# One loop of single tiles, in place of a tree of conditions, for an expert's tokens past its first 128

## The chip, the cores and the metric

The kernel runs on one core of a Trainium2 chip. The metric is the device time of one execution in microseconds, from the first instruction to the end. Inputs and outputs lie in device memory, and all tokens are routed on the chip.

## The reference

Three parts follow one another. First an attention with a position bias (4 batches, 8 heads, 576 positions, head size 64). Then a dense two-layer network with a SiLU-like gate. Last a mixture of eight experts, and only this part is touched:

```python
do_compute = x @ w_skip > 0                 # 2304 tokens of 512 features
e_idx  = argmax(xc @ w_gate)                # one expert per token
gate_w = softmax(xc @ w_gate)[e_idx]
h      = maximum(xc[mask] @ w1[e], 0)       # 512 -> 1024
y      = gate_w * (h @ w2[e])               # 1024 -> 512
out    = xc + y                             # other tokens: out = x
```

How many tokens an expert gets is known only at run time. The kernel must work for any count.

## The kernel before

All matrix work of the experts is done in pairs of 16-bit numbers: a value is split into a high and a low half (`xh`, `xl`; `Wh`, `Wl`; `hh`, `hl`), and three of the four products are summed. So a tile of 128 tokens takes, for each of eight slices `f` of the hidden layer, twelve matmuls of 128 columns (L547), then a ReLU on ScalarE (L554) and the low half on VectorE (L555), and, two slices later (`MLAG`), three matmuls of 512 columns (L563). With the four transposes of the next expert's tokens (`spread`, L523) that makes 124 matmuls. A matmul is two instructions of TensorE, a weight load and the multiplication.

The stage order is written by hand from `tail` on (`manual_schedule`): each engine runs its instructions in program order. `experts` (L626) goes through the eight experts. The first 128 tokens of an expert are one tile with a hook, `between`, that puts other work between its slices: the previous tile's end (`finish`, L581 and L582: gate and residual on VectorE, then a scatter by POOL into `out`), the fetch of later tokens by POOL (L504), the split of the next expert's weights in eight pieces (`piece`, L497 on ScalarE and L498 on VectorE), and the issue by SP of the loads of later weights (`load`, L481 and L483; two transfers of 256 KB for a piece, into a ring of 16, so a load waits until the piece 16 places earlier has been split). All engines get the expert's count as a number of half tiles, `n[e]` (L648); SP gets it too and takes its own branches, and so runs ahead of the others.

Tokens past the first 128 are handled by a tree of conditions (L669 to L697). `n == 3` runs a half tile (`expert_half`), `n == 4` a second full tile (`second`), `n > 4` fetches three more tiles and runs the second tile with a spread of these, then either a double tile and a half (`n == 9`) or a triple tile and, past ten, a loop over four tiles at a time. For experts 0 and 7 the second tile's tokens are already transposed ahead of the condition (`SY0`, `SY7`). In the listing of the compiled program the tree takes about 1,750 instructions of TensorE for each expert: 241 to 246 for the half tile, as many for the second full tile, 257 to 261, 529 and 338 for the larger ones, and 404 for the loop's body. Where a condition fails, an engine jumps over its block to a few instructions that add to its counters what the block would have counted; POOL does this for its transfers with one counter instruction (INC_SWDGE_SEM) after waiting for its earlier transfers.

A loop over a number known only at run time (`tc.For_i`) is written by the framework as follows, and the loop at L693, which this run does not reach, is in the listing. The first pass is entered directly. Between two passes stands a block in which SP waits for the counters of every engine and of every DMA queue, all five engines meet in a join, each takes back its counters (POOL by the same kind of counter instruction), they meet in a second join, and the body begins again. After the last pass each of the five engines goes through 13 instructions that wait for the counters of all engines and DMA queues, those of earlier loads among them, before it goes on.

## Time and profile before

| | us |
|---|---|
| median of 3 runs (999.99 to 1008.25) | 1003.2 |
| the profiled execution | 1003.57 |
| its span | 1001.5 |
| TensorE busy | 814.1 (81%) |
| VectorE busy | 701.9 (70%) |
| ScalarE busy | 531.4 (53%) |
| POOL busy | 77.1 (8%) |

The profile is one execution. Its page splits the span into 40 slices, the last eight of which hold the experts. Busy time of TensorE (PE) is the time in which a matmul was in its pipeline; PEld is the weight load beside it. A row of a timeline gives start, duration, engine, line, operation, output and inputs, how many instructions were merged, and in brackets the idle time before and what ended it; "PEq L669" there is the branch at L669 on TensorE's sequencer. DVE is VectorE, ACT is ScalarE. A row by stretch gives its start and end, its length, the busy time of PE, PEld, DVE, ACT and POOL with the number of instructions, the granted TensorE clock as a share of full speed, the DMA engines' busy share, and GB/s.

### The profile page before, as it was taken

How to read it: one execution, taken by the hardware profiler on the slowest of the kernel's cores; microseconds unless marked ns; L12 is line 12 of the kernel's file. 1: busy time of each engine (PE TensorE's matmuls, PEld its weight loads, DVE VectorE, ACT ScalarE, POOL GpSimd, SP SyncE). 2: the span in 40 equal slices, each digit the busy share in tenths (PEclk: the TensorE clock that was granted, in tenths of full speed). 3: DMA queues.
4: the chain of work that ended last, by engine and by line, in shares of the span. 5: the costliest groups of instructions: out<-in, count | busy, mean ns of one | idle time of the engine just before them, and what ended most of it. 6: DMA issues, size and time to landing. Idle time of an engine off the chain costs nothing. (4 is left out here: it accounts for less than half of the span.)

```text
span 1001.5 us, 21950 instructions
## 1 busy us (share of the span) xinstructions
PE 814.1 (81%) x8074; PEld 534.0 (53%) x8074; DVE 701.9 (70%) x1989; ACT 531.4 (53%) x1067; POOL 77.1 (8%) x98
## 2 busy tenths in 40 slices
PE   5656598578679999988897999999989775778973
PEld 1212254364375757475745556756674554656652
DVE  6798898889964778677666877776776555672251
ACT  5555566574653657466555656656563344662140
POOL 1110011000000000000000000000001221120010
PEclk9788999799889999999999999999989898788998
DMA  7999999999995899999979998979697769860010
GB/s 195 244 289 262 261 290 220 265 248 253 274 208 111 192 182 221 215 219 203 198 157 181 215 219 189 214 152 205 124 267 234 217 216 291 251 196 13 24 29 15
DMA packets 357238, 199.25 MB, mean 199 GB/s; under 512 B 263900, under 2 KB 319580, under 8 KB 357088
## 3 DMA queue, kind: packets, MB, share of 16 engines
q1 hardware_dynamic: 350112, 178.84, 78.5%
q0 software_dynamic: 6160, 17.97, 6.2%
q8 instruction: 82, 1.34, 0.6%
q10 hardware_dynamic: 816, 0.54, 0.2%
q14 instruction: 68, 0.56, 0.2%
HBM read 113.52 MB, written 24.19 MB: 138 GB/s over the span
## 5 line engine op out<-in xcount | busy, mean ns | idle before, releaser
L280 PE MATMUL hps<-x,win 128*128 128x192 f16 x2304 | 213.3, 251 | 7.3 <-DVE th L284 5.8
L300 PE MATMUL ops<-wout,g 128*128 128x512 f16 x864 | 203.3, 385 | 9.7 <-ACT wout L267 6.8
L280 PEld LDWEIGHTS <-win 128*128 128x128 f16 x2304 | 191.0, 99 | 19.9 <-issue 11.1
L217 ACT ACTIVATE e<-e,st 128x576 f32<-128x576 f32 x144 | 111.0, 771 | 79.7 <-DVE st L215 74.8
L300 PEld LDWEIGHTS <-g 128*128 128x128 f16 x864 | 79.9, 99 | 101.5 <-issue 13.0
L222 DVE SCALAR_TENSOR_TENSOR en<-e,st,en 128x576 f16<-128x576 f32 x144 | 116.9, 815 | 24.1 <-ACT en L221 23.2
L212 PE MATMUL sc<-kT,qT 128*64 128x512 f16 (+1 forms) x1152 | 108.0, 305 | 29.2 <-ACT bs L140 15.2
L221 ACT ACTIVATE en<-e,st 128x576 f16<-128x576 f32 x144 | 110.0, 768 | 27.6 <-ACT e L217 15.3
L215 DVE CUSTOM_DVE_ANT_0 e<-sc,bt 128x576 f32<-128x576 f32 x144 | 108.3, 752 | 18.7 <-PE sc L212 10.3
L547 PEld LDWEIGHTS <-W 128*128 128x128 f16 x1056 | 80.7, 110 | 56.1 <-issue 35.2
L212 PEld LDWEIGHTS <-qT 128*64 128x64 f16 x1152 | 58.7, 114 | 87.5 <-issue 61.0
L235 PE MATMUL av<-eT,vh 128*64 128x192 f16 x864 | 68.2, 253 | 44.5 <-DMA eT<-en 41.9
L137 PE MATMUL bps<-hh,hb 128*32 128x64 f32 (+1 forms) x576 | 77.0, 660 | 26.8 <-ACT bs L140 10.2
L235 PEld LDWEIGHTS <-vh 128*64 128x64 f16 x864 | 50.4, 112 | 55.6 <-issue 37.2
L547 PE MATMUL h<-xh,W 128*128 128x128 f16 x512 | 47.5, 246 | 32.4 <-PEq L669 24.0
L428 POOL DMA_INDIRECT slots<-ent x18 | 19.4, 1077 | 580.5 <-DVE ent L427 458.9
L137 PEld LDWEIGHTS bps<-hh,hb 128*32 128x32 f32 x576 | 19.6, 125 | 82.2 <-issue 50.8
L131 DVE TENSOR_SCALAR hh<-pos 128x576 f32<-128x576 f32 x120 | 55.4, 516 | 7.5 <-PE bps L137 7.4
L288 ACT ACTIVATE g<-th 128x384 f16<-128x384 f32 x96 | 48.4, 514 | 22.6 <-DVE th L284 22.6
L284 DVE SCALAR_TENSOR_TENSOR th<-th,hps 128x384 f32<-128x384 f32 x96 | 52.1, 548 | 7.6 <-ACT th L283 7.2
L289 DVE SCALAR_TENSOR_TENSOR g<-th,g 128x384 f16<-128x384 f32 x96 | 52.2, 552 | 2.8 <-ACT g L288 2.0
L283 ACT ACTIVATE th<-hps 128x384 f32<-128x384 f32 x96 | 45.5, 479 | 14.6 <-PE hps L280 12.2
(150 smaller groups left out, 1080.7 us busy)
## 6 DMA issues: line engine op xcount, KB each, us to landing
bt<-bias_d SPq DMA_DIRECT2D x144, 288.0 KB, 3.5
win<-in_moe_w SPq DMA_DIRECT2D x48, 256.0 KB, 6.3
wout<-in_moe_w SPq DMA_DIRECT2D x46, 256.0 KB, 5.5
bias_d<-bs POOLq DMA_DIRECT2D x36, 288.0 KB, 5.2
wr<-in_moe_w_in SPq DMA_DIRECT2D x16, 512.0 KB, 5.7
wr<-in_moe_w_out SPq DMA_DIRECT2D x16, 512.0 KB, 4.7
qr<-in_q SPq DMA_DIRECT2D x48, 96.0 KB, 3.9
x2s<-x SPq DMA_DIRECT2D x36, 128.0 KB, 2.5
```

Source lines behind the costliest of these rows:

```text
L131: nc.vector.tensor_scalar(hh, src, self.bl[:, j : j + 1], 0.0, op0=ALU.add, op1=ALU.max)
L137: nc.tensor.matmul(ps[32 * c : 32 * c + 32, ks], self.w2b, v.rearrange("q (p n) -> q n p", n=4) if ks.start == 0 else v, start=True, stop= ...
L212: nc.tensor.matmul(o, qT[:, w, i, js], k_, start=(w == 0), stop=(w == 1))
L215: nc.vector.tensor_tensor_reduce(out=e, in0=sc[:, :S], in1=bt, scale=1.0, scalar=3.0e38, op0=ALU.add, op1=ALU.min, accum_out=st4[:, 0:1])
L217: nc.scalar.activation(e, e, AF.Exp, bias=st4[:, 0:1], scale=-1.0, accum_out=st4[:, 1:2])
L221: nc.scalar.activation(en[:, 0], e, AF.Copy, scale=st4[:, 2:3])
L222: nc.vector.scalar_tensor_tensor(out=en[:, 1], in0=e, scalar=st4[:, 2:3], in1=en[:, 0], op0=ALU.mult, op1=ALU.subtract)
L235: nc.tensor.matmul(av[js], v_[:, j, kb], eT[:, :, kb, js], start=(n == 0), stop=(n == len(seq) - 1))
L280: nc.tensor.matmul(ps[:, u], self.win[w][:, k, fs], x[:, k], start=(i == 0), stop=(i == 11))
L289: nc.vector.scalar_tensor_tensor(out=gl, in0=th, scalar=XS / (2 * XS * WS), in1=gh, op0=ALU.mult, op1=ALU.subtract)
L300: nc.tensor.matmul(ps, self.g[gi][:, fb, d], self.wout[w][:, fb, :], start=(n == 0), stop=(n == 47))
L547: nc.tensor.matmul(h, w[:, f, 0, 128 * k : 128 * k + 128], v[:, k], start=(i == 0), stop=(i == 11))
```

## The change

The tree of conditions goes, with `expert_half`, the wide forms of `expert_tile`, the buffers for these (`yb`, `xqb`, `hqb`) and the early spreads of experts 0 and 7. In its place stands one condition with one loop, whose body handles one tile of 128 tokens. Each pass transposes the tokens in `xn`, keeps a copy of them (`xk`) and of their rows and gates (`idk`), loads the next tile's rows from `slots` into `idq`, fetches its tokens into `xn`, computes, and scatters. The high and low halves of the tokens lie side by side in `xc`, so that one matmul of 256 columns multiplies a weight by both; the two results are added by a copy on ScalarE and an addition on VectorE. With the transposes a pass has 92 matmuls, 184 instructions of TensorE.

```diff
-        self.yb = [m.tile([128, 4, 128], F16, name=f"y{i}", bufs=1) for i in range(2)]
...
+        at = lambda o, n, dt: g1[:, o : o + n].bitcast(dt)
+        self.more = (m.tile([128, 2], I32, name="idq", bufs=1), m.tile([128, 2], I32, name="idk", bufs=1), at(0, 1024, F32),
+                     g1[:, 1024:2048].rearrange("p (k v c) -> p k v c", k=4, v=2), [at(2048 + 256 * i, 256, F32) for i in range(3)],
+                     *([g1[:, 2816 + 128 * (2 * i + v) : 2944 + 128 * (2 * i + v)] for i in range(3)] for v in range(2)))
...
+    def expert_more(self, e, ids, n, xn):
+
+        nc, tc, m = self.nc, self.tc, self.m2
+        Wh, Wl = self.W[e]
+        idq, idk, xk, xc, hs, hh, hl = self.more
+        j = 2 * (e * SL + 1)
+        slots = self.slots.rearrange("(p n) c -> p (n c)", p=128)
+        with tc.If(n > 2):
+            nc.vector.tensor_copy(idq, ids[:, j : j + 2])
+            with tc.For_i(2, n, 2) as i:
+                xp = self.ps.tile([128, 1024], F32, tag="sc", name="xp", bufs=SCB)[:, :512].rearrange("p (k c) -> p k c", k=4)
+                for k in range(4):
+                    nc.tensor.transpose(xp[:, k], xn[:, 128 * k : 128 * k + 128], self.ident)
+                nc.scalar.activation(xc[:, :, 0], xp, AF.Copy, scale=XS)
+                nc.vector.scalar_tensor_tensor(out=xc[:, :, 1], in0=xp, scalar=XS, in1=xc[:, :, 0], op0=ALU.mult, op1=ALU.subtract)
+                nc.gpsimd.tensor_copy(xk, xn)
+                nc.gpsimd.tensor_copy(idk, idq)
+                nc.gpsimd.dma_start(idq, slots[:, ds(i + j, 2)])
+                self.fetch1(idq[:, 0:1], xn)
+                y = self.ps.tile([128, 1024], F32, tag="sc", name="y", bufs=SCB)[:, :DM]
+                for f in range(8 + MLAG):
+                    if f < 8:
+                        h = self.ps.tile([128, 2, 128], F32, tag="mm", name="h", bufs=MMB)
+                        for k in range(4):
+                            nc.tensor.matmul(h, Wh[:, f, 0, 128 * k : 128 * k + 128], xc[:, k], start=(k == 0), stop=False)
+                        for k in range(4):
+                            nc.tensor.matmul(h[:, 0], Wl[:, f, 0, 128 * k : 128 * k + 128], xc[:, k, 0], start=False, stop=(k == 3))
+                        q = f % 3
+                        nc.scalar.activation(hs[q], h[:, 1], AF.Copy)
+                        nc.vector.tensor_tensor(hs[q], h[:, 0], hs[q], op=ALU.add)
+                        nc.scalar.activation(hh[q], hs[q], AF.Relu)
+                        nc.vector.scalar_tensor_tensor(out=hl[q], in0=hs[q], scalar=0.0, in1=hh[q], op0=ALU.max, op1=ALU.subtract)
+                    if f >= MLAG:
+                        g, q = f - MLAG, (f - MLAG) % 3
+                        for p, w in ((hh, Wh), (hh, Wl), (hl, Wh)):
+                            nc.tensor.matmul(y, p[q], w[:, g, 1], start=(g == 0 and p is hh and w is Wh), stop=(g == 7 and p is hl))
+                nc.vector.scalar_tensor_tensor(out=xk, in0=y, scalar=idk[:, 1:2].bitcast(F32), in1=xk, op0=ALU.mult, op1=ALU.add)
                 nc.gpsimd.indirect_dma_start(
+                    out=self.out, out_offset=bass.IndirectOffsetOnAxis(ap=idk[:, 0:1].bitcast(U32), axis=0),
+                    in_=xk, in_offset=None, bounds_check=NT - 1, oob_is_err=False)
...
@@ experts
-                if e in (0, NE - 1) and f == (SY7 if e else SY0):
-                    st["y"] = self.spread([xm[e]], "y")
...
-            with tc.If(n[e] > 2):
...
-            st.pop("y", None)
+            self.expert_more(e, ids, n[e], xm[e])
```

## Rows read from the trace of the kernel before

**Rows 1.** Stages of the experts: length, busy us by engine, granted clock, DMA share

```profile
796.20:811.77 15.57, 10.88 (x120) 7.66 (x121) 4.52 (x11) 2.63 (x9) 3.25 (x4) 1.00 0.84 265
811.77:833.36 21.59, 12.74 (x125) 9.38 (x126) 12.29 (x18) 9.81 (x18) 5.87 (x5) 0.87 0.76 236
...
869.81:888.88 19.07, 14.03 (x124) 10.31 (x125) 12.40 (x18) 10.36 (x18) 2.92 (x3) 0.77 0.87 258
...
902.08:950.65 48.57, 41.86 (x401) 29.96 (x401) 13.34 (x30) 9.10 (x25) 2.97 (x3) 0.93 0.05 18
950.65:969.54 18.89, 13.14 (x124) 9.30 (x125) 13.12 (x19) 9.94 (x17) 4.56 (x4) 0.91 0.14 39
969.54:980.52 10.98, 10.98 (x124) 8.14 (x125) 3.03 (x9) 2.82 (x9) 0.00 (x0) 1.00 0.02 4
980.52:1001.50 20.98, 5.68 (x121) 4.11 (x119) 3.41 (x7) 1.11 (x4) 1.89 (x2) 0.76 0.05 17
```

**Rows 2.** Branches and counters by line: count, ns min/median/max; TensorE's waits

```profile
L669 PEldq COMPARE_BRANCH  x8: 70/4250/6136, 794.9 to 979.1; - x8
...
L669 POOLq INC_SWDGE_SEM  x5: 1478/1602/1902, 826.4 to 963.0; - x5
...
  PE h L547: 24.0, 5
...
L673 PEldq COMPARE_BRANCH  x4: 71/270/353, 795.0 to 984.2; - x4
...
L675 PEldq COMPARE_BRANCH  x4: 68/205/3135, 796.4 to 984.4; - x4
```

**Rows 3.** Timeline of TensorE at the start of expert 3

```profile
851.52 0.98 PE L547 MATMUL h<-xh,W 128*128 128x128 f16 x8 [4.59 <-PEq L669]
...
855.81 0.61 PE L547 MATMUL h<-xh,W 128*128 128x128 f16 x8
```

**Rows 4.** VectorE's groups from 850 us on: count, busy us, mean ns, idle

```profile
L498 DVE SCALAR_TENSOR_TENSOR W<-wout,W 128x1024 f16<-128x1024 f32 x16 | 19.5, 1221 | 7.4 <-ACT W L497 7.1
...
L555 DVE SCALAR_TENSOR_TENSOR hl<-h,hh 128x128 f16<-128x128 f32 x40 | 11.5, 288 | 11.3 <-ACT hh L554 11.3
L581 DVE SCALAR_TENSOR_TENSOR g<-y,ids,g 128x512 f32<-128x512 f32 x8 | 5.9, 750 | 6.1 <-PE y L563 5.7 <-PEq L690 0.4
...
L526 DVE SCALAR_TENSOR_TENSOR xl<-xp,xh 128x512 f16<-128x512 f32 x4 | 2.7, 683 | 0.0
```

**Rows 5.** Timeline of SP, first of 14 issues up to 802.37

```profile
793.46 0.38 SPq L481 DMA_DIRECT2D wout<-in_moe_w  x1
```

**Rows 6.** One stretch of 10 us, columns as in the first group

```profile
840.00:850.00 10.00, 6.85 (x65) 4.28 (x61) 7.05 (x11) 4.70 (x9) 1.69 (x2) 1.00 1.04 316
```

**Rows 7.** Timeline of all engines in expert 0's second tile

```profile
795.91 0.58 POOL L642 DMA_DIRECT2D ids<-slots  x1 [2.04 <-DMA slots<-ent]
...
797.09 1.56 PE L547 MATMUL h<-y,W 128*128 128x128 f16 x25 [0.91 <-DVEq L673]
...
801.82 0.99 POOL L504 DMA_INDIRECT g<-x2s,ids  x1 [5.33 <-DMA ids<-slots]
```

**Rows 8.** Issue to landing: of the fetch L504, then the scatter L582

```profile
DMA to landing us min/median/max: 3.3/4.3/7.0
...
DMA to landing us min/median/max: 2.2/3.1/5.8
```

**Rows 9.** Timeline of TensorE at the start of expert 5's second tile

```profile
905.97 0.88 PE L523 MATMUL xp<-ident,g 128*128 128x128 f32 x4 [3.88 <-PEq L675]
907.58 4.00 PE L547 MATMUL h<-y,W 128*128 128x128 f16 x36 [0.74 <-ACT y L525]
```

**Rows 10.** POOL's groups over the span, columns as for VectorE's

```profile
L345 POOL MEMSET sen<- 128x352 int32 x1 | 0.4, 392 | 0.0
```

**Rows 11.** Timeline of POOL at the end

```profile
988.05 0.91 POOL L622 DMA_INDIRECT out<-g,ids  x1 [5.31 <-DVEq L675]
```

## The prediction

> **What bounds the kernel now.** I read the chain of waits first. It goes back only a few experts and names little but "issue", so I went on to a table by stage [rows 1] and to each stage's timeline. The change touches only the last 205 us, where the eight experts run one behind the other. Each expert streams one tile of 128 tokens: 124 matmuls, 10.98 us where nothing disturbs them (969.54 to 980.52). Experts 1 to 4 take 77.1 us together (811.77 to 888.88; four stages, first and last shown, 21.59 and 19.07 us). VectorE is busy for only about 12 us of each, and the DMA engines for 0.76 and 0.87 of it, so neither fills a stage. What ends the idle time on TensorE is the branch of the outer `If` (L669): five waits, 24.0 us [rows 2]. That branch lasts 70 ns where it falls through (the minimum) and 4.25 (the median of all eight) to 6.14 us where it is taken and jumps over the whole tree, some 1,750 TensorE instructions in the listing of the program. After such a gap TensorE is granted the lower clock for a while: eight matmuls take 0.98 us at 851.52 and 0.61 us at 855.81 [rows 3]. From 851.52 to 855.81 it does three groups of twelve matmuls of 128 columns and one of three of 512. A tile at the full clock has eight of each, 1,536 columns a group, and the transposes in 10.98 us: 0.66 us a group, 2.6 for four. About 1.6 us are lost.

> Which experts have more than 128 tokens is read from the stages: expert 0 runs a second full tile (n = 4, 15.57 us), expert 5 the branch n = 9 (48.57 us), expert 7 a half tile (n = 3). The other five skip. So the change is a trade: five cheaper skips against one, four and one passes of the new loop.

> **Skips, experts 1 to 4.** The new block holds 92 matmuls, 184 TensorE instructions and about 30 for the loop's ends, so the skip jumps some 215. The nearest rows are L673 and L675, which jump over 241 to 246: 0.2 to 0.35 us, once 3.14 us, right behind another jump [rows 2]. I take 0.4 us, and 3.1 us as the upper bound. With the gap gone VectorE sets the pace: per expert 8 pieces of 1.22 us, 8 hl of 0.288, one xl of 0.683 and one finish of 0.750, 13.5 us [rows 4]; with hand-overs I take 14.0. The clock then stays up, except in expert 1, which follows a loop: 14 x 4 + 1.5 = 57.5 us against 77.1, a gain of 19.6.
> What could be late next is the weights. SP, which ran ahead, now has to join expert 0's loop. The seven pieces it issued from 793.46 on (the row is the first of 14 issues [rows 5]) go out only after that loop, and 24 more must land before expert 5's tile ends: 31 x 0.524 MB = 16.2 MB. At the 316 GB/s of one 10 us stretch [rows 6] that is 51 us, at the 258 GB/s of a whole stage 63. There are some 70 us until then, so I take nothing, and 5 us as the bound, since each expert's share has its own due time.

> **Expert 6.** Its stage of 18.89 us holds one skip of about 4 us and a slow start; at VectorE's pace it becomes 15: a gain of 3.9.

> **Expert 0's pass.** The first instruction in the new block is VectorE's copy of `idq` out of `ids`. That transfer is issued at 795.91 and lands 5.7 us later; today only POOL's fetch waits for it, until 801.82 [rows 7]. VectorE works in order, so the low half of xc stands behind this copy, and every first matmul reads both halves. Today the second tile starts at 797. Now: copy until 802.0, xc 0.68, start at 802.7. The body streams the same columns as a tile does (per f: 4 x 256 + 4 x 128 for 12 x 128), 10.5 us without the transposes, plus 1.8 at the low clock: 815.0. Then 0.2 + 0.75 (gate) + 0.25 until POOL's scatter starts, 2.7 until it lands (the scatter's row has 2.2 to 5.8, median 3.1, beside heavy traffic [rows 8]; without SP's loads I take below the median), and the exit, where every engine goes through 13 waits: 1.0. That is 819.9 against 811.77: a loss of 8.2. Removing the early spread of xm saves under 0.5 us of TensorE.

> **The cost of a pass.** No loop runs in the trace of before, so its join is bounded. What hides nothing: the next pass may not start until the scatter has landed, since the join waits for all DMAs. Per pass: lead 2.3 us (transposes at 905.97 to the first matmul at 907.58 are 1.6 [rows 9], plus 0.68 for the low half that this body needs at once); body 10.5; low clock 1.6; gate and hand-overs 1.2; landing 2.7; join 3.3. The join is one POOL counter instruction of 1.48 to 1.90 us [rows 2], which stands between the two joins, and 1.7 for SP's row of waits and both joins. Low bound 1.5 (that instruction alone), high bound 5. Sum 21.6 us.
> POOL's copy of xn has no row; POOL's largest plain write takes 0.39 us [rows 10], and I allow 0.4 to 3. The load of idq (5.7 at most, by the row of `ids`) and the fetch of the next tile (1.0, and 4.3 to land [rows 8]) follow it. That makes 11 to 14 us beside the 14 of lead, body and low clock, so nothing, or 1 us a pass. The four small operations per f (ScalarE, VectorE, ScalarE, VectorE, each within 0.29) make a chain of 1.3 us, while its reader comes 1.3 to 2.6 us later: nothing, at most 1 us a pass.

> **Expert 5.** First pass 20.6 (little low clock), three of 21.6, less 2.3 because the last ends in the exit: 83.1 us against 48.57, a loss of 34.5. The matmuls themselves hardly grow (41.9 us busy now, 44 then); the loss is four leads, three joins, four landings.

> **Expert 7.** From 980.52 to its scatter at 988.05 [rows 11] it takes 7.5 us; then 0.1 + 2.0 + 10.5 + 1.2 = 13.8. A loss of 6; what follows the scatter I leave as it is (a join comes, two counter instructions go).

> **Sum.** -19.6 - 3.9 + 8.2 + 34.5 + 6.0 = +25.2 us. The profiled execution took 1003.57 us (span 1001.5), 0.4 above the median of the three runs, so 1003.2 + 25.2 = 1028.

> [...] On the rows, a jump over 1,750 instructions costs 4 to 6 us and one over 245 mostly 0.2 to 0.35 [rows 2]. [...] No run here shows a jump back; what it would do is the first rival.

> **Rivals.**
> *Fetches stay* (0.18). TensorE's jump back reaches for code that has gone, and short skips cost what L675's dearest did. For: that row's maximum. Against: the medians of both rows of short jumps. Price: five skips x 2.7 = 13.5. A fetch at a jump back of 3.1 to 6.1 us runs beside the 4 to 7 us of gate, landing and join, so 3 x 1.5 = 4.5. 1028 + 18 = 1046.
> *Cheap joins* (0.13). Each landing at 2.2, join at 1.5, no low clock: 3.9 less in three of expert 5's passes, 1 to 2 less in each of the other three, experts 1 to 4 at 13.5: about -17, 1011.
> *Passes overlap: faster or level* (0.09). Place: the end of a pass in expert 5. If an engine could go on before the scatter has landed, the transposes of the next tile and POOL's fetch would run behind the gate, and a pass would cost lead and body, 13.5. Expert 5: 4 x 13.5 + 3 = 57 (+8.5); expert 0 without landing and exit +4.5; expert 7 +5; against -23.5: -5.5, 998. With the pace at VectorE's bare 13.5 us and a shorter lead it comes under 993. It decides where a pass falls below 15 us. Against: the joins wait for every DMA.

> **Numbers.** Forecast 0.60 (its own range 1016 to 1040), and 0.18, 0.13, 0.09 for the three. About 1% (993 to 1013) is what a measurement here can tell from no change. Faster: 0.05, out of the overlap. Within: 0.10, 0.04 of the overlap and 0.06 of the cheap joins. Slower: 0.85. The range 1010 to 1046 takes in the bounds of join, landing and fetch.

> **What would show it.** The five skips at 0.2 to 0.5 us, and experts 1 to 4 at 14 us each with VectorE over 90% busy. TensorE idle for 7 to 10 us between expert 5's passes, ended by a join, with starts 21 to 22 us apart. Expert 0's first loop matmul at 802 to 803. Expert 7's scatter 14 us after its tile. The forecast is wrong if the passes are under 15 us apart, if the skips still cost 3 us, or if ScalarE or VectorE waits in experts 2 to 4 for weights.

## The result: slower by 1.0%, where 2.5% was forecast

The changed kernel takes 1016.26 us (median of 4 runs, 1014.80 to 1017.45), the kernel before 1003.50 (four runs): a ratio of 1.0102, 95% interval 1.0059 to 1.0144. The sign was forecast, the size was not: 1016 lies in the range given, but 12 us under the 1028 of the forecast. The profiled execution has a span of 1014.7 us, 13.2 more than before. Ratios go by undisturbed runs; of the traces below only that of a_drain is of a run in the slower state.

The head of the page after; all of the growth is between 795 us and the end:

```profile
span 1014.7 us, 22246 instructions
PE 830.2 (82%) x7978; PEld 539.0 (53%) x7978; DVE 717.4 (71%) x2054; ACT 548.6 (54%) x1131; POOL 91.8 (9%) x119
```

The stage table of the changed kernel, columns as in [rows 1]: expert 0's pass, experts 1 to 4, expert 5's own tile, three of its four passes, expert 6, expert 7's tile, and expert 7's pass with the end.

```profile
795.62:816.79 21.17, 12.89 (x93) 8.41 (x92) 6.97 (x21) 5.67 (x19) 5.96 (x8) 0.86 0.21 55
816.79:830.61 13.82, 13.44 (x125) 9.96 (x125) 12.43 (x19) 10.19 (x18) 4.49 (x3) 0.84 0.96 298
830.61:843.73 13.12, 11.98 (x125) 7.88 (x126) 12.34 (x19) 10.00 (x18) 2.94 (x3) 1.00 1.10 335
843.73:856.79 13.06, 11.97 (x124) 7.87 (x125) 12.06 (x19) 9.98 (x18) 3.00 (x3) 1.00 1.09 339
856.79:869.83 13.04, 11.98 (x125) 7.90 (x126) 12.08 (x19) 10.00 (x18) 2.96 (x3) 1.00 1.08 338
869.83:887.66 17.83, 13.60 (x124) 9.73 (x125) 12.37 (x19) 10.16 (x17) 3.74 (x5) 0.81 1.09 338
887.66:910.40 22.74, 11.27 (x93) 7.60 (x93) 5.93 (x18) 5.07 (x17) 2.61 (x4) 0.84 0.14 43
910.40:931.00 20.60, 13.60 (x93) 9.17 (x93) 6.12 (x18) 5.29 (x17) 3.31 (x6) 0.83 0.08 26
...
951.54:971.95 20.41, 13.52 (x93) 9.12 (x94) 6.45 (x19) 5.89 (x18) 3.29 (x5) 0.83 0.06 19
971.95:985.44 13.49, 12.77 (x124) 9.34 (x125) 12.22 (x19) 9.54 (x17) 3.81 (x2) 0.89 0.13 42
985.44:996.40 10.96, 10.96 (x124) 8.16 (x125) 3.05 (x10) 2.22 (x8) 1.00 (x1) 1.00 0.02 5
996.40:1014.70 18.30, 10.80 (x90) 7.12 (x88) 6.54 (x20) 5.07 (x17) 4.35 (x6) 0.94 0.10 32
```

Set beside [rows 1], and with the two scatters (988.05 before [rows 11], 1009.76 after) to part the last stage:

| term | forecast | measured | miss |
|---|---|---|---|
| expert 0's pass, up to expert 1's start (811.77 before, 816.79 after) | +8.2 | +5.0 | -3.2 |
| experts 1 to 4 (77.1 before, 53.0 after) | -19.6 | -24.1 | -4.5 |
| expert 5's own tile (13.2 before, 17.8 after) | 0 | +4.6 | +4.6 |
| expert 5's rest (48.6 before, 84.3 after) | +34.5 | +35.7 | +1.2 |
| expert 6 | -3.9 | -5.4 | -1.5 |
| expert 7, tile's end to its scatter (7.5 before, 13.4 after) | +6.0 | +5.8 | -0.2 |
| from that scatter to the end (13.45 before, 4.94 after) | 0 | -8.5 | -8.5 |
| sum | +25.2 | +13.2 | -12.0 |

The misses add up to -17.9 us and to +5.8 us, and cancel in part; that 1016 lies inside the range given is in part this luck.

The skips went as said. In the view of the line of the outer condition (columns: smallest, median, largest ns; first and last start), the branch has fallen from a median of 4250 ns [rows 2] to 344 (of all eight, three of which are not taken):

```profile
L575 PEldq COMPARE_BRANCH  x8: 70/344/466, 794.5 to 995.0; - x8
```

TensorE's waits by releaser (total us, times, longest): the five skips now cost 1.6 us against 24.0, and the passes' joins (L577) 21.2.

```profile
PE xp L580 <- PEq L577: 21.2, 3, 10.1
...
PE h L592 <- DVE g L582: 10.4, 6, 3.3
...
PE h L538 <- issue: 8.9, 2, 5.0
PE h L538 <- SPq L631: 5.5, 1, 5.5
...
PE h L538 <- PEq L575: 1.6, 5, 0.4
```

The largest miss is the end. POOL's DRAINs at the line of the kernel's end (L912 before, L863 after; the largest is the third number), and inside the new loop (L577):

```profile
L912 POOLq DRAIN  x3: 46/251/7421, 992.8 to 1001.2; - x3
```

```profile
L863 POOLq DRAIN  x3: 40/102/881, 1012.9 to 1014.5; - x3
```

```profile
L577 POOLq DRAIN  x6: 47/1486/7852, 901.5 to 951.1; - x6
```

Before, a drain of 7.42 us stands alone at the end, with two counter instructions of 1.95 and 1.97 us ahead of it (the third number of each row):

```profile
L675 POOLq INC_SWDGE_SEM  x2: 1706/1828/1949, 891.7 to 988.2; - x2
...
L677 POOLq INC_SWDGE_SEM  x2: 1430/1698/1965, 813.0 to 990.6; - x2
```

After, the last scatter starts at 1009.76:

```profile
1009.76 1.00 POOL L605 DMA_INDIRECT out<-g,idk  x1 [6.75 <-DVE g L604]
```

The drain at the end now takes 0.88 us, and one of 7.85 us stands in the loop's first join, at 901.5. There it shows in POOL's timeline as the wait ahead of the copy that opens the second, third and fourth pass:

```profile
910.37 0.61 POOL L583 COPY g<-g 128x512 f32<-128x512 f32 x1 [7.87 <-POOLq L577]
...
930.98 0.61 POOL L583 COPY g<-g 128x512 f32<-128x512 f32 x1 [3.41 <-POOLq L577]
...
951.51 0.61 POOL L583 COPY g<-g 128x512 f32<-128x512 f32 x1 [3.41 <-POOLq L577]
```

TensorE stood idle for 10.06 us ahead of the second pass and for 5.59 ahead of the third and fourth. So the drain costs 4.5 us there, the rest of it running beside the scatter's landing (2.7 us, the median of L605), and saves 6.5 us at the end.

### The profile page after: what moved, and what is told of

Same layout as the page of the kernel before. It is cut to its first block, busy times and chain, and to the rows that moved or that the text cites. A ratio compares the mean times of both kernels' runs of the same rounds, so it can differ in the third digit from the quotient of the medians.

```text
span 1014.7 us, 22246 instructions
## 1 busy us (share of the span) xinstructions
PE 830.2 (82%) x7978; PEld 539.0 (53%) x7978; DVE 717.4 (71%) x2054; ACT 548.6 (54%) x1131; POOL 91.8 (9%) x119
## 5 line engine op out<-in xcount | busy, mean ns | idle before, releaser
L215 DVE CUSTOM_DVE_ANT_0 e<-sc,bt 128x576 f32<-128x576 f32 x144 | 108.2, 752 | 20.6 <-PE sc L212 11.2
L235 PE MATMUL av<-eT,vh 128*64 128x192 f16 x864 | 71.9, 261 | 46.8 <-DMA eT<-en 44.2
L235 PEld LDWEIGHTS <-vh 128*64 128x64 f16 x864 | 52.7, 116 | 57.8 <-issue 40.2
L538 PEld LDWEIGHTS <-W 128*128 128x128 f16 x768 | 52.9, 106 | 29.0 <-issue 17.9
L288 ACT ACTIVATE g<-th 128x384 f16<-128x384 f32 x96 | 48.4, 514 | 22.7 <-DVE th L284 22.7
L538 PE MATMUL h<-xh,W 128*128 128x128 f16 x512 | 43.9, 234 | 16.8 <-issue 8.9
```

The source lines that it names most:

```text
L215: nc.vector.tensor_tensor_reduce(out=e, in0=sc[:, :S], in1=bt, scale=1.0, scalar=3.0e38, op0=ALU.add, op1=ALU.min, accum_out=st4[:, 0:1])
L235: nc.tensor.matmul(av[js], v_[:, j, kb], eT[:, :, kb, js], start=(n == 0), stop=(n == len(seq) - 1))
L538: nc.tensor.matmul(h, w[:, f, 0, 128 * k : 128 * k + 128], v[:, k], start=(i == 0), stop=(i == 11))
```

## The experiments

A name that begins with b_ is a variant of the kernel before, one with a_ of the changed kernel. Each ratio is to the kernel before in the runs beside it (its medians there are 1005.7 to 1007.6 us), with the 95% interval in brackets.

**Where POOL's drain is paid.** Theory: POOL's first drain after software transfers is dear wherever it stands, and the tree's kernel pays it at its end. Rival: the long end came from the tree's own code there.

A drain put early into the kernel before, where POOL has nothing urgent (b_drain), and the same into the changed one (a_drain):

```diff
                 self.x0 = self.fetch1(idl.rearrange("p a b -> p (a b)")[:, 0:1], self.xnb[0])
+                self.nc.gpsimd.drain()
```

> The kernel before with one addition: POOL is drained once at about 771 us, when it has nothing to do. Theory 1 (the first drain of POOL after its transfers costs about 7 us once, wherever it stands; the kernel before pays 7.4 us of it at its very end, after 992.8): the early drain lasts about 7 us and hides, the last drain falls below 1 us, and the kernel takes 6 to 7 us less, about 997. Theory 2 (a drain costs about 0.1 us for each software transfer since the one before it): 36 of 77 are left, the last drain takes 3.5 us, and the kernel takes 3 to 4 us less. Rival (the long drain at the end waits for the last scatter or for the counter instructions ahead of it): nothing changes at the end, 1003, or up to 3 us more.

> The changed kernel with the same single drain of POOL at about 771 us. Theory 1: the first pass of expert 5, 22.7 us, becomes as long as the others (20.5), since its join no longer holds the first drain of 7.9 us; the end stays as it is; 1014. Theory 2: about 30 transfers are left, 3 us, which the landing of the scatter hides: also 20.5 and 1014. Rival (the first join is long because code has to be fetched or because weights are still landing): 22.7 stays, 1016.

b_drain: 1000.18 us, ratio 0.9949 (0.9915 to 0.9982), span 994.9. The early drain takes 9.58 us beside other work, and the one at the end falls from 7.42 to 2.92 us:

```profile
L858 POOLq DRAIN  x1: 9584/9584/9584, 767.1 to 767.1; - x1
```

```profile
L913 POOLq DRAIN  x3: 52/164/2923, 990.8 to 994.6; - x3
```

That nothing would change is refuted. Neither theory fits in full: the gain of some 5 us (0.5%) lies between the two, and 2.92 us are nearer theory 2's 3.5 than the "below 1" of theory 1. The counter instructions at L669 shrank too, from a median of 1602 ns [rows 2] to 502:

```profile
L669 POOLq INC_SWDGE_SEM  x5: 378/502/802, 821.3 to 959.6; - x5
```

a_drain: 1012.11 us, ratio 1.006 (1.0021 to 1.0099), by the intervals not to be told from the changed kernel; the longest drain in the loop falls from 7.85 to 3.93 us and the first gap between passes from 10.06 to 6.16:

```profile
L577 POOLq DRAIN  x6: 52/1483/3934, 907.1 to 952.9; - x6
```

Next the loop itself was taken away: the body written straight into the condition and run once (a_single). It leaves out expert 5's last 384 tokens.

```diff
-            with tc.For_i(2, n, 2) as i:
+            for i in (2,):
...
-                nc.gpsimd.dma_start(idq, slots[:, ds(i + j, 2)])
+                nc.gpsimd.dma_start(idq, slots[:, i + j : i + j + 2])
```

> The changed kernel with the loop's body written straight into the condition, run once, and no loop at all: expert 5's last 384 tokens are left out. No engine joins before the kernel's end. Theory 1, POOL's first drain after its software transfers costs some 7 to 8 us wherever it stands, and the changed kernel's end is short only because expert 5's first back-edge has paid it: the last POOL drain lasts 7 to 8 us, and from expert 7's scatter to the end it is 12 to 13.5 us (4.9 in the changed kernel, 13.45 in the kernel before). Rival, the end was long before because of the tree's code at the end (the jump and the two counter instructions): the drain stays under 2 us, the end at 5 to 6.5. Expert 0's part without the loop's exit: expert 1's first matmul within 1.2 us of the last one of expert 0 (4.96 with it). By the span, 1014.7 less about 62 (three passes of expert 5), less 8 (two exits and expert 5's), plus 8: 950 to 957.

One execution: 948.28 us, span 946.5, 3.5 us below the range expected. The drain is back at the end, with 8.24 us; from the scatter (937.20) to the end it is 9.3 us, the drain and 1 us around it, and not 12 to 13.5: the two counter instructions that I had counted in are the tree's.

```profile
L863 POOLq DRAIN  x3: 46/113/8237, 937.4 to 946.2; - x3
```

So the drain's place, not the tree's code, made the 6.5 us; this is one execution, and b_drain and a_drain agree with it. Two drains in the kernel before (b_drain2) asked whether its length goes by the transfers since the last one:

```diff
+                if e == 6 and f == 2:
+                    nc.gpsimd.drain()
```

> The kernel before with two POOL drains ahead of the end: one right after its first fetch, as in the run that gained 6 us, and one in expert 6's tile. Theory 1, a drain's length goes by the software transfers issued since the last one: the one in expert 6 lasts some 2.5 to 3 us, and the last one at the end falls from 2.92 to under 1 us. Rival, only the first drain of a kernel is dear and each later one has a floor of its own: the end stays at 2.9. Span 992 to 995 by the first, 995 to 998 by the second.

One execution, 997.17 us. The last drain falls to 0.30 us, as theory 1 said, but the one in expert 6 lasted 6.72 us and not 3, and the span is 995.1, no shorter than with one drain. So a drain that is not the first can be dear too. That a later drain always has a floor of 2.9 us is refuted; what sets the length of a drain (the transfers issued, or those on their way, a scatter and a fetch of 957 to 960 us) is not settled.

```profile
L915 POOLq DRAIN  x3: 52/103/301, 993.6 to 994.8; - x3
```

```profile
L652 POOLq DRAIN  x1: 6716/6716/6716, 957.6 to 957.6; - x1
```

**What makes a skip cheap.** In a_far, 750 dead matmuls that never run stand behind the loop, so a skip jumps far again:

```diff
+            with tc.If(n > 35):
+                far = self.ps.tile([128, 1024], F32, tag="sc", name="far", bufs=SCB)[:, :DM]
+                for i in range(750):
+                    nc.tensor.matmul(far, hh[0], Wh[:, i % 8, 1], start=(i == 0), stop=(i == 749))
```

> The changed kernel with 750 matmuls more behind the loop, in a condition (n > 35) that never holds, so that a skip jumps over some 1,710 instructions of TensorE in place of 208. If the gain at the five skips is the length of the jump: each of the five costs 4 to 6 us again, experts 1 to 4 take 17.5 to 18.5 us apiece in place of 13.1, and with the three experts that now jump over the dead block (3 to 5 us each) the kernel takes 25 to 40 us more, 1041 to 1056. If the gain came from elsewhere (weights, the order of VectorE's work): experts 1 to 4 stay at 13.1, and only the three jumps add 9 to 15 us.

1060.32 us, ratio 1.0548 (1.0486 to 1.0609), 4 us above the range expected. The five skips cost TensorE 24.7 us (24.0 in [rows 2]), by the length of the jump alone:

```profile
L575 PEldq COMPARE_BRANCH  x8: 70/4322/5588, 795.0 to 1033.9; - x8
```

In b_hint the tree stays. The count is read at slice 3 of the tile, and TensorE is told there which way the outer condition will go. b_early is its control: the early read without the hint.

```diff
-                if f == NLF:
+                if f == (NLF if e == 0 else 3):
                     n.append(nc.values_load(...))
+                    tc.mark_branch_hint_location(f"more{e}", hint=n[e] > 2, engines=[ENG.PE])
...
-            with tc.If(n[e] > 2):
+            with tc.If(n[e] > 2, label=f"more{e}"):
```

> The kernel before with its tree untouched. For experts 1 to 7 the count is read at the fourth slice in place of the last, and TensorE's sequencer is told there, by a hint that reads the count, whether the outer branch will be taken (for expert 0 just ahead of the branch). If the 4 to 6 us of a skip are a fetch of code from a place far away: the five skips fall to 0.2 to 0.5 us, experts 2 to 4 take 13 to 14 us apiece, and the kernel takes 16 to 24 us less, 980 to 987. If they are something else that the jump does: nothing changes, 1003. If reading the count early or the hint delays TensorE's own stream: 1 to 4 us more.

> The kernel before with its tree, each expert's count read at slice 3 of its tile and not after the last one, and no hint: the control of the run that gained 20 us with both. Theory 1, the five skips cost TensorE a fetch of far code, which begins when the branch is executed, so reading the count earlier changes nothing: the five waits at L669 stay at 22 to 25 us in sum, and the time stays within 1% of before. Rival, part of the gain came from the count being there sooner: the waits fall to 10 to 18 us and the time to 0.985 to 0.99 of before.

b_hint: 983.58 us, ratio 0.9795 (0.9736 to 0.9853). b_early: 1005.60 us, ratio 1.0 (0.9968 to 1.0031). TensorE's wait at the skips goes from 24.0 us to 1.8 with the hint, and stays at 24.5 without. A part of the gain is spent elsewhere: ahead of experts 1 and 6 TensorE now waits 6.5 and 5.2 us for split weights, and expert 2 took 17.1 us, not 13 to 14 (experts 3 and 4 took 13.4 and 14.0). First b_hint, then b_early:

```profile
PE h L547 <- DVE W L498: 11.7, 2, 6.5
...
PE h L547 <- PEq L670: 1.8, 2, 1.6
```

```profile
PE h L547 <- PEq L669: 24.5, 5, 5.9
```

So a skip is dear where the jump is long and its way not told (24.0 us for the five, 24.7 in a_far), and telling the sequencer ahead brings it down to 1.8 as the short block does to 1.6, with no pass made dearer. Both cheap edits in one kernel (b_hint_drain, the tree untouched):

> The kernel before with its tree, with both small edits that gained each by itself: TensorE is told ahead which way the outer condition of experts 1 to 7 goes, and POOL drains once right after its first fetch. If the two gains lie in different places (five skips, and the drain at the kernel's end), they add: 983.6 - 6 = 977 to 979 us, 0.973 of before, the last POOL drain under 3 us. If the drain at the end is only hidden by something else once the skips are short, or costs elsewhere: 982 to 985.

982.89 us, ratio 0.9766 (0.9715 to 0.9818), span 976.5 against 980.9 with the hint alone. The last drain is 2.92 us. This kernel is faster than the kernel before and the changed one; by the intervals it can't be told from b_hint. The median lies in the range of the second theory, the profiled run, with 978.23 us the fastest of six, in that of the first; so whether the two gains add is open.

**The stop in expert 5's own tile.** Nothing in the forecast stood for the 4.6 us there. The timeline of TensorE shows a stop with no wait behind it ("issue"), 1 us and 16 matmuls into the tile:

```profile
869.83 0.61 PE L538 MATMUL h<-xh,W 128*128 128x128 f16 x8 [0.31 <-PEq L575]
...
874.82 0.59 PE L538 MATMUL h<-xh,W 128*128 128x128 f16 x4 [3.94 <-issue]
```

a_light asks whether traffic makes it, and whether transfers or VectorE set the pace of experts 1 to 4. Its edit leaves out the loads of the second weight matrix from piece 40 on, which are experts 5 to 7, and not 4 to 7 as the text ahead of the run says:

```diff
-        q.dma_start(r[:, 1], self.a["moe2_w2"][e, fs, :])
+        if p < 40:
+            q.dma_start(r[:, 1], self.a["moe2_w2"][e, fs, :])
```

> The changed kernel, which leaves out the loads of the second weight matrix of experts 4 to 7 (their split then works on what lies in the ring; the output differs). It takes a half of the traffic away that fills the DMA engines (share 1.08 at 335 to 339 GB/s) during experts 1 to 4. Theory 1, VectorE sets the pace of these stages: they stay at 13.0 to 13.1 us with the DMA share at 0.6 to 0.8. Rival, the transfers set it: they shorten to 11 to 12 us. And on the 3.94 us that TensorE stands still 5 us into expert 5's own tile with no wait in the profile: if it is a fetch of code that queues behind the weights, it falls to 2 us or less; if it is the fetch itself, it stays at 3 to 4. Time by theory 1 with the shorter fetch 1011 to 1014 us, with the long one 1014 to 1017, by the rival 1006 to 1010.

1018.22 us, ratio 1.0112 (1.0041 to 1.0182). The traffic gets lighter only late: expert 2 still has 335 GB/s, expert 3 has 308 (339 in the changed kernel), expert 4 has 240 (338). Expert 4 doesn't get faster, so transfers don't set its pace; for experts 1 to 3 this run can't tell. Experts 3 and 4 get slower, from 13.05 to 14.47 us, with VectorE as busy as before; so VectorE's work alone doesn't set it either. Expert 2, with its traffic unchanged, went from 13.12 to 13.96 us too, so the slowing can't be put to the lighter traffic, and why the hand-overs lengthened is open.

```profile
827.01:840.97 13.96, 11.98 (x125) 7.87 (x125) 12.51 (x19) 9.81 (x18) 2.93 (x3) 1.00 1.09 335
840.97:855.44 14.47, 12.13 (x124) 7.92 (x125) 12.26 (x19) 9.89 (x18) 2.99 (x3) 1.00 1.13 308
855.44:869.91 14.47, 11.97 (x125) 7.88 (x126) 12.26 (x19) 9.92 (x18) 2.97 (x3) 1.00 0.87 240
```

The stop comes 1.05 us into the tile as before (869.91 to 870.96) and lasts 2.69 us, between the two figures expected, while the DMA share over that tile is down from 1.09 to 0.22. So traffic may lengthen the stop, but does not make it. The taken branches of the kernel before fit this: four last 4.8 to 6.1 us beside the weight loads (share 0.76 to 0.89 over their stages), the one ahead of expert 7 3.7 us (share 0.14); that was not tried by itself. So a_pad moves the code: 16 dead matmuls in expert 0's tile shift all that follows by 33 instructions.

```diff
+                if e == 0 and f == 5:
+                    pad = self.ps.tile([128, 128], F32, tag="mm", name="pad", bufs=MMB)
+                    for i in range(16):
+                        nc.tensor.matmul(pad, self.W[0][0][:, 0, 0, :128], ...)
```

> The changed kernel with 16 dead matmuls (33 TensorE instructions, some 1.3 us) put into expert 0's first tile, so that all code behind them lies 33 instructions later. [...] Rival, the stop belongs to the traffic or to what expert 5 does at that time: it stays at 3.5 to 4.5 us, 1 us into expert 5's tile. Time 1013 to 1018 by both, so the trace decides.

1016.66 us, ratio 1.0115 (1.005 to 1.018): the same time, and the stop is elsewhere. It is gone from expert 5's tile; 2.39 us stand ahead of it, at the skip, and 2.85 us in expert 2's tile, 48 matmuls (49 weight loads, 97 instructions) behind its start at 831.26:

```profile
837.43 0.33 PE L538 MATMUL h<-xl,W 128*128 128x128 f16 x3 [2.85 <-issue]
...
875.54 0.61 PE L538 MATMUL h<-xh,W 128*128 128x128 f16 x8 [2.39 <-PEq L575]
```

So the stop belongs to a place in the code: in the changed kernel it came behind 16 matmuls and 17 weight loads, 33 instructions into expert 5's tile, and 33 instructions more bring it to the tile's start. What happens at such a place, and why it costs 2.4 to 3.9 us, no run shows.

**What a pass of the loop costs.** a_inline writes the first extra tile straight into the condition and keeps a loop only for the further ones:

```diff
-            with tc.For_i(2, n, 2) as i:
+            def one(i):
...
+            one(2)
+            with tc.If(n > 4):
+                with tc.For_i(4, n, 2) as i:
+                    one(i)
```

> The changed kernel, with the first extra tile of an expert written out straight in the condition and only the further ones (n > 4) in a loop inside it; so experts 0 and 7 pass no loop end, and expert 5 has one pass less in the loop. Theory 1, a loop's entry and end are what a pass costs beyond its body: expert 1's first matmul, which came 4.96 us after expert 0's last loop matmul, comes within 1 us of it (-4); expert 5's first long gap of 10.06 us between passes goes, but the long POOL drain moves to the next back-edge, whose gap grows from 5.6 to about 10 (-5 to -6 in sum); the end shortens by 1 to 2; skips of experts 1 to 4 and 6 now jump twice as far (some 400 to 430 instructions) and cost up to 1 us each (+0 to +3). Sum about -9: 1005 to 1009 us. [...] Theory 3, the landing of the scatter and not the loop's end holds expert 1 and expert 5: no gap shrinks, 1014 to 1018.

1025.56 us, ratio 1.0199 (1.0127 to 1.0272): above the ranges of theories 1 and 3 in the time (1005 to 1009, 1014 to 1018), and as theory 1 said in the places where the loop went. Expert 1's first matmul comes 1.07 us after expert 0's last (4.96 in the changed kernel). The long drain moved to what is now the first back-edge, with 10.31 us, where 10 were expected. But a skip of some 390 instructions is dear in two of four experts (5.65 us in the second row) and leaves a stop in the next tile in the other two (5.09 in the first, 4.45 at 864.13):

```profile
827.08 1.04 PE L538 MATMUL h<-xh,W 128*128 128x128 f16 x8 [5.09 <-issue]
844.90 1.01 PE L538 MATMUL h<-xh,W 128*128 128x128 f16 x8 [5.65 <-PEq L575]
...
932.41 1.11 PE L580 MATMUL xp<-ident,g 128*128 128x128 f32 x4 [10.31 <-PEq L611]
```

a_stag writes the loop with staggered counters in place of the join:

```diff
-            with tc.For_i(2, n, 2) as i:
+            with tc.For_i(2, n, 2, iteration_sync="staggered") as i:
```

> The changed kernel, whose loop is written with staggered counters: the body is cut into four stages, and an engine may enter a stage once the others have left the one before the last, so that there is no join of all engines between passes. Theory 1, the join is what keeps passes apart (5.6 us of idle TensorE, of which some 3 are the scatter's way and 2.5 the join): expert 5's passes go from 20.5 to 15 to 18 us, its stretch from 84.3 to 62 to 74, the kernel to 1002 to 1008 us. Theory 2, the stages' own waits cost as much (each stage ends in waits of all engines, four a pass): passes stay at 19 to 22 us with TensorE's idle time spread inside the body, 1012 to 1020 us. The long POOL drain of 7.85 us at the first back-edge has no place left before the loop's exit; by the theory that it must be paid at POOL's first drain it appears at the kernel's end, and the end grows by about 6.

1015.19 us, ratio 1.0082 (1.0044 to 1.012), no different from the change. The trace is of a run of 1023.05 us, the longest of the ten. The starts of the last three passes, and the first matmul of expert 6:

```profile
916.40 0.65 PE L580 MATMUL xp<-ident,g 128*128 128x128 f32 x4 [1.86 <-issue]
934.51 0.65 PE L580 MATMUL xp<-ident,g 128*128 128x128 f32 x4 [1.85 <-issue]
953.79 0.65 PE L580 MATMUL xp<-ident,g 128*128 128x128 f32 x4 [1.84 <-issue]
972.60 0.62 PE L538 MATMUL h<-xh,W 128*128 128x128 f16 x8 [2.48 <-PEq L577]
```

The passes are 18 to 19 us apart, against 20.5. The gap of 5.59 us became one of 1.85 and 3.4 more inside (1.41 before) until the first product: ScalarE's copy of the tokens, which the product needs, starts only when the scatter has landed.

```profile
919.05 0.60 ACT L581 ACTIVATE g<-xp 128x512 f16<-128x512 f32 x1 [5.41 <-DMA out<-g,idk]
```

That is theory 2, with a small gain. The gain is given back: experts 1 to 4 take 57.3 us, not 53.0, and expert 0's pass begins after 6.18 us of idle TensorE. The drain at the end took 3.33 us, not the 7.85 of the changed kernel's first join, and the end grew by 0.9 us, not by 6: this loop issues 27 counter instructions (L577, 178 to 1397 ns), the changed kernel's loop 3; whether they take over what the drain costs was not tried by itself.

## Why the prediction was wrong

**The step that failed** is the last words of the paragraph on expert 7: "what follows the scatter I leave as it is (a join comes, two counter instructions go)". It set 0 and measured -8.5 us, more than two thirds of the miss. Up to the scatter the same paragraph was right to 0.4 us (13.8 said, 13.4 measured). Behind it, the tree's kernel paid a POOL drain of 7.42 us and two counter instructions of 3.9, and the changed kernel 0.88 and none; that is 10.5 us, of which some 2 come back because the changed kernel's drain starts only at 1012.9, 3.1 us behind the scatter's start. The loop's first join had paid the drain, 4.5 us of it in the open. What sets a drain's length stays open. a_single, which has no join, shows the drain back at the end (8.24), a_inline shows it moved to its own first join (10.31 us of gap), and b_drain shows that an early one takes 4.5 us from the end even without the change. The trace of before held this: the 20.98 us of the last stage [rows 1] with 13.45 of them behind the last scatter [rows 11], though a scatter lands in 3.1 us [rows 8]. The 10 us between were not asked for a cause.

**Experts 1 to 4** (-19.6 said, -24.1 measured). The mechanism was right: the skips cost 0.3 to 0.4 us, and a_far (24.7 us for the five) and b_hint (1.8) show that what they paid was the length of a jump whose way was not told ahead. (A taken branch lasted 3.7 to 6.1 us before; the 4.25 of the prediction is the median of all eight, three of them not taken.) The size was off in the pace: I added durations of VectorE to 13.5 us and put 0.5 on top, but its instructions overlap at their ends: one starts some 0.08 us before the one ahead of it is over (in expert 2, 831.53 + 1.24 = 832.77 against 832.69). The sum of its rows is 13.5 us while VectorE was busy for 12.1 to 12.3, and the stages took 13.05; that VectorE sets this pace is not shown (a_light). Expert 6 follows the same way.

**Expert 0** (+8.2 said, +5.0 measured). From its first product to expert 1 the pass took 17.25 us, 17.2 were said. The 3.2 us are the wait for `ids`: it landed in 2.6 us, not 5.7. My own text had the reason, that SP now has to wait for this loop and its loads go out later, but I used it only for the weights. In a_single there is no loop to wait for, `ids` is issued at 798.86 and lands 5.9 us later, and the first product starts at 805.61, which fits; that it was SP's traffic was not tried by itself. First the changed kernel, then a_single:

```profile
798.37 0.17 DVE L576 COPY idq<-ids 128x2 int32<-128x2 int32 x1 [1.87 <-DMA ids<-slots]
```

```profile
804.80 0.17 DVE L576 COPY idq<-ids 128x2 int32<-128x2 int32 x1 [7.20 <-DMA ids<-slots]
```

**Expert 5's passes** (+34.5 said, +35.7 measured) were right in sum by luck, through two errors: the gaps are 5.59 us, and the starts 20.5 us apart, not 21.6; the first gap is 10.06 us, for the drain. No row had shown the 1.7 us set for SP's waits and both joins, nor a join as a whole (3.3). From the scatter's start (926.56) to the next pass's transposes (931.00) it took 4.4 us, some 2.7 of them its landing, so 1.7 by this estimate for the whole join, whose counter instruction took 0.22 us and not 1.48 to 1.90.

**Expert 5's own tile** (0 said, +4.6 measured) is a stop of 3.94 us that belongs to a place in the code (a_pad). All branches of the loop cost TensorE 80 to 304 ns; the stop came one tile further on.

**The rivals.** "Fetches stay" is refuted: the five skips cost 1.6 us in all, and the loop's branches, those back among them, 80 to 304 ns each. "Cheap joins" has nearly the measured time, by other terms: the passes took 20.5 us and not under 18, and the end did the rest. "Passes overlap" is refuted: every pass waits for the join, and without the join (a_stag) passes come only 1 to 2.5 us closer.

## What to carry to other kernels

Account for the end of a kernel like any stage: the time from the last transfer's landing to the last instruction is a term, and a change that adds or removes an earlier join can move it. Before code is rewritten to shorten a jump, try to tell the engine the branch's way ahead of time: it gained 2% here (1.5 to 2.6), with the tree untouched. And when a new wait holds one engine back, go through every transfer that this engine no longer competes with.
